# Attention and token mixing on one core: q/k transposes moved to VectorE, 32-row scores, fixed order, resident loads

## The chip, the cores and the metric

The kernel runs on one core of a Trainium2 chip. The metric is the device time of one execution in microseconds (us). A run is called fast when it lies within 1.5% of the fastest run of the same kernel, else slow. This kernel's runs scatter by some per cent (the kernel before: 195.8 to 204.7 us in the rounds of the experiments, at mean granted TensorE clocks of 0.88 to 0.96), so I compare fast runs with fast runs where there are enough of them, and say so where a median includes slow ones.

Engine names as in the profile: PE is TensorE's matmuls, PEld its weight loads, DVE is VectorE, ACT is ScalarE, POOL is GpSimd (which issues the loads), SP is SyncE (which issues the stores of the new kernel; in the kernel before ScalarE does). L12 is line 12 of the kernel in question. The line numbers of the two kernels differ.

## The reference

```python
# q, k, v: (8 batches, 8 heads, 576 rows, 64), float32; attention within chunks of 64 rows
scores = matmul(q_c, k_c.T) / sqrt(64)            # per batch, head, chunk: 64 x 64
x = softmax(scores) @ v_c                         # -> (8, 576, 512), heads side by side
wq, wk = x @ w_q, x @ w_k                         # (8, 576, 64)
mixed = (wq @ wk.T / sqrt(64)) @ x                # (8, 576, 512)
out = relu(mixed) @ w_out                         # float32
```

Both kernels compute `mixed` as `wq @ (wk.T @ x)`; I call `wk.T @ x` "g" (64 x 512). The inputs are random, with a standard deviation of 0.1 for q and k, so scores are small and the softmax is nearly flat. Therefore the comparison with the reference hardly notices wrong scores (experiment 6 shows it).

## The kernel before

Per batch, per pair of heads: load rows as they lie, transpose q and k on PE, scores, exp, attention times v, scaling. The token mixing of the batch before is cut into pieces and put between the head pairs; a scheduler then orders each engine's instructions. All of the token mixing shares two PSUM banks, the pool with tag "m".

```python
    st_psum = ... bufs=2      # scores            (8 PSUM banks used in all)
    x_psum  = ... bufs=2      # attention times v
    t_psum  = ... bufs=2      # q/k transposes
    m_psum  = ... bufs=2      # all of the token mixing, tag "m"
    ...
    # load: q/k rows of 64 elements (256 bytes in DRAM), one DMA per 128 positions
    nc.gpsimd.dma_start(res[ti][0:rows, j], src[b][:, ds(j * P, rows), :].rearrange("h p d -> p h d"))
    ...
            for ti in range(2):                       # q, then k
                tp = t_psum.tile([P, NJ, P], F16, name=f"tp{ti}", tag="tp")
                for j in range(NJ):
                    nc.tensor.transpose(tp[:, j, 0:rows], qn[ti][0:rows, j, 2 * hp : 2 * hp + 2, :], ident[0:rows, 0:rows])
                sb = qkt_pool.tile(...)
                nc.vector.tensor_copy(sb[:], tp...)
            ...
                        nc.tensor.matmul(stp[r0 : r0 + CH, ci, :], lhsT=kt[r0 : r0 + CH, cs], rhs=qt[r0 : r0 + CH, cs])  # 64 rows
    ...
        def p_mixed():
            for i in range(NDC):                      # four pieces
                ma = m_psum.tile([P, 512], F32, name="ma", tag="m")
                mb = m_psum.tile([P, CH], F32, name="mb", tag="m")
                ...                                   # two matmuls, two relus on ScalarE
        def p_out():                                  # five a batch, the last of 64 rows
                op = m_psum.tile([P, DM], F32, name="op", tag="m")
                ...                                   # four matmuls, copy, store
```

The softmax here doesn't subtract the row's maximum and nothing guards it: scores larger than these inputs give would overflow.

## Time and profile before

Median 197.88 us of 4 runs (197.22 to 201.69). From the page of the profiled execution, which spans 195.1 us: the share of each engine, and, in 40 slices, PE's busy tenths and the granted clock.

```profile
span 195.1 us, 4950 instructions
...
PE 165.3 (85%) x2064; PEld 91.6 (47%) x2064; DVE 80.7 (41%) x272; ACT 77.9 (40%) x193; POOL 117.1 (60%) x153
...
PE   0249987999889989988989999999999998975691
...
PEclk9999998557999699999999999999987999998559
...
PE 70%; DMA 10%; ACT 9%; POOL 4%; DVE 4%; issue 2%; POOLq 0%; ACTq 0%; DVEq 0%
```

The last line is the chain that ended last, by engine. The windows of the middle (columns: the stretch, its length, then busy us of PE, PEld, DVE, ACT, POOL, then clock, DMA share and GB/s):

```profile
100.00:120.00 20.00, 19.45 (x275) 11.30 (x275) 10.49 (x38) 9.97 (x25) 17.52 (x23) 1.00 1.89 170
120.00:140.00 20.00, 19.77 (x287) 11.60 (x286) 10.93 (x38) 9.62 (x26) 7.14 (x10) 1.00 1.08 119
```

A matmul counts as busy for its whole duration, about 0.19 us for one of 64 columns although the next may start some 20 ns later (the scores matmuls between 75 and 150 us). So a wait shorter than that leaves no idle time.

Two groups of the page (columns: line, engine, operation, shapes, count; busy us and mean ns; idle time before, and its releaser):

```profile
L188 PE MATMUL op<-wout_133,rmx 128*128 128x512 f16 (+1 forms) x160 | 46.6, 432 | 1.0 <-ACT rmx L174 1.0
...
L174 ACT ACTIVATE rmx<-ma 128x512 f16<-128x512 f32 x32 | 19.2, 600 | 12.2 <-PE mb L173 11.1
```

And PE's wait for the relu of the mixed pieces, from the list of waits (who waited for whom: us in total, times, longest):

```profile
PE ma L172 <- ACT rmx L174: 3.7, 8, 0.7
```

### The profile page before, as it was taken

How to read it: one execution, taken by the hardware profiler on the slowest of the kernel's cores; microseconds unless marked ns; L12 is line 12 of the kernel's file. 1: busy time of each engine (PE TensorE's matmuls, PEld its weight loads, DVE VectorE, ACT ScalarE, POOL GpSimd, SP SyncE). 2: the span in 40 equal slices, each digit the busy share in tenths (PEclk: the TensorE clock that was granted, in tenths of full speed). 3: DMA queues.
4: the chain of work that ended last, by engine and by line, in shares of the span. 5: the costliest groups of instructions: out<-in, count | busy, mean ns of one | idle time of the engine just before them, and what ended most of it. 6: DMA issues, size and time to landing. Idle time of an engine off the chain costs nothing.

```text
span 195.1 us, 4950 instructions
## 1 busy us (share of the span) xinstructions
PE 165.3 (85%) x2064; PEld 91.6 (47%) x2064; DVE 80.7 (41%) x272; ACT 77.9 (40%) x193; POOL 117.1 (60%) x153
## 2 busy tenths in 40 slices
PE   0249987999889989988989999999999998975691
PEld 0127742445545446544655475556554654442230
DVE  0025840453745337433846275618640764160000
ACT  2002213433326533563338543661464326623432
POOL 8999996999999997799799499703000000000000
PEclk9999998557999699999999999999987999998559
DMA  5999999999999999999999999975002300240015
GB/s 36 133 134 95 152 155 125 100 145 207 216 171 141 108 205 223 138 119 212 229 144 147 226 162 151 133 230 61 5 0 110 127 12 0 90 155 0 0 64 178
DMA packets 119749, 24.56 MB, mean 126 GB/s; under 512 B 114608, under 2 KB 115120, under 8 KB 119728
## 3 DMA queue, kind: packets, MB, share of 16 engines
q0 software_dynamic: 114480, 14.82, 117.6%
q10 hardware_dynamic: 5248, 9.44, 13.7%
q8 instruction: 16, 0.26, 0.6%
q14 instruction: 5, 0.04, 0.1%
HBM read 29.62 MB, written 9.44 MB: 200 GB/s over the span
## 4 chain that ended last, share of the span: by engine, by line
PE 70%; DMA 10%; ACT 9%; POOL 4%; DVE 4%; issue 2%; POOLq 0%; ACTq 0%; DVEq 0%
PE op L188 17%; DMA out_dram<-osb 8%; PE ma L172 7%; PE tx L109 6%; PE gp L154 6%; PE wpa L120 4%; ACT rmx L174 3%; DMA qn_102<-in_q_dram 2%; POOL qn_102 L72 2%; ACT osb L196 2%; ACT wqkT L135 2%; POOL qn_103 L72 2%; PE wknp L145 2%; DVE x_nat L281 1%; PE wpb L127 1%
## 5 line engine op out<-in xcount | busy, mean ns | idle before, releaser
L83 POOL DMA_DIRECT2D vt<-in_v_dram x64 | 47.7, 807 | 15.7 <-PE stp_2655 L245 7.7
L188 PE MATMUL op<-wout_133,rmx 128*128 128x512 f16 (+1 forms) x160 | 46.6, 432 | 1.0 <-ACT rmx L174 1.0
L196 ACT COPY osb<-op 128x512 f32<-128x512 f32 (+1 forms) x40 | 23.3, 583 | 33.1 <-PE op L188 25.8
L188 PEld LDWEIGHTS <-rmx 128*128 128x128 f16 (+1 forms) x160 | 16.0, 110 | 19.8 <-issue 9.6
L174 ACT ACTIVATE rmx<-ma 128x512 f16<-128x512 f32 x32 | 19.2, 600 | 12.2 <-PE mb L173 11.1
L270 PEld LDWEIGHTS <-est 64*64 64x64 f16 x640 | 15.8, 115 | 11.2 <-issue 4.7
L109 PE MATMUL tx<-ident,x_nat 128*128 128x128 f16 x160 | 14.9, 231 | 4.7 <-ACT osb L196 1.8
L109 PEld LDWEIGHTS <-x_nat 128*128 128x128 f16 x160 | 10.2, 101 | 7.2 <-issue 4.4
L135 ACT CAST wqkT<-wpa 128x512 f16<-128x512 f32 x8 | 4.7, 585 | 19.5 <-PE wpb L127 19.5
L154 PE MATMUL gp<-x_nat,wkn 128*64 128x512 f16 (+1 forms) x40 | 11.4, 389 | 1.2 <-DVE wkn L149 1.2
L223 PE MATMUL tp_192<-ident,qn_102 128*128 128x128 f16 (+1 forms) x5 | 1.4, 277 | 6.9 <-DMA qn_102<-in_q_dram 6.8
L177 ACT ACTIVATE rmx<-mb 128x64 f16<-128x64 f32 x32 | 7.2, 224 | 0.0
L154 PEld LDWEIGHTS <-wkn 128*64 128x64 f16 (+1 forms) x40 | 3.5, 107 | 6.5 <-DVE wkn L149 1.6
L223 PEld LDWEIGHTS <-qn_102 128*128 128x128 f16 (+1 forms) x20 | 1.9, 115 | 8.9 <-DMA qn_102<-in_q_dram 7.6
L252 ACT ACTIVATE est<-stp_209 128x320 f16<-128x320 f32 x1 | 0.4, 437 | 13.0 <-PE stp_209 L245 13.0
L72 POOL DMA_DIRECT2D qn_136<-in_k_dram x5 | 5.4, 1085 | 0.0
L72 POOL DMA_DIRECT2D qn_135<-in_q_dram x5 | 5.4, 1081 | 0.0
L229 DVE COPY qkt_198<-tp_192 128x576 f16<-128x576 f16 x1 | 0.5, 458 | 11.9 <-PE tp_192 L223 11.9
L145 PE MATMUL wknp<-ident,wqkT 64*128 64x64 f16 (+1 forms) x40 | 3.4, 196 | 2.0 <-ACT wqkT L135 1.8
L72 POOL DMA_DIRECT2D qn_1309<-in_k_dram x5 | 4.4, 873 | 1.2 <-DMA vt<-in_v_dram 1.2
L149 DVE COPY wkn<-wknp 128x256 f16<-128x256 f16 x8 | 2.3, 288 | 6.5 <-PE wknp L145 6.4
L72 POOL DMA_DIRECT2D qn_102<-in_q_dram x5 | 4.5, 904 | 0.3 <-issue 0.3
(656 smaller groups left out, 384.0 us busy)
## 6 DMA issues: line engine op xcount, KB each, us to landing
out_dram<-osb ACTq DMA_DIRECT2D x32, 256.0 KB, 4.0
vt<-in_v_dram POOLq DMA_DIRECT2D x64, 72.0 KB, 4.5
out_dram<-osb ACTq DMA_DIRECT2D x8, 128.0 KB, 3.7
qn_102<-in_q_dram POOLq DMA_DIRECT2D x4, 128.0 KB, 4.0
qn_103<-in_k_dram POOLq DMA_DIRECT2D x4, 128.0 KB, 4.2
wout_133<-in_moe_w_out_dram POOLq DMA_DIRECT2D x1, 512.0 KB, 6.3
qn_135<-in_q_dram POOLq DMA_DIRECT2D x4, 128.0 KB, 6.4
qn_136<-in_k_dram POOLq DMA_DIRECT2D x4, 128.0 KB, 6.4
```

Source lines behind the costliest of these rows:

```text
L72: nc.gpsimd.dma_start(res[ti][0:rows, j], src[b][:, ds(j * P, rows), :].rearrange("h p d -> p h d"),)
L83: nc.gpsimd.dma_start(vt[CH * hh : CH * hh + CH, :, 0:CH], v[b, 2 * hp + hh].rearrange("(c kk) d -> kk c d", kk=CH),)
L109: nc.tensor.transpose(tx[:, j, :], x_nat[:, j, ts(i, P)], ident[:])
L120: nc.tensor.matmul(pa[:, :], lhsT=wqk16[:, i, :], rhs=xts[i][:, 0:512], start=(i == 0), stop=(i == NDC - 1),)
L135: nc.scalar.copy(wqkT[:, 0:512], pa[:, :])
L145: nc.tensor.transpose(wknp[0:rows, j, :], wkT[:, ds(j * P, rows)], ident[CH:P, CH:P])
L154: nc.tensor.matmul(gp[:, :], lhsT=wkn[0:kk, j, :], rhs=x_nat[0:kk, j, :], start=(j == 0), stop=(j == NJ - 1),)
L172: nc.tensor.matmul(ma[:, :], lhsT=g16[:, ts(i, P)], rhs=wqT[:, 0:512])
L174: nc.scalar.activation(rmx[:, i, 0:512], ma[:, :], AF.Relu, scale=scale_moe)
L188: nc.tensor.matmul(op[0:m, :], lhsT=rmx[:, i, ds(st * P, m)], rhs=wout16[:, i, :], start=(i == 0), stop=(i == NDC - 1),)
L196: nc.scalar.copy(osb[0:m, :], op[0:m, :])
L270: nc.tensor.matmul(xp[hh][half : half + CH, sl // 2, 0:65], lhsT=est[r0 : r0 + CH, c, :], rhs=vt[r0 : r0 + CH, c, 0:65], start=True, stop= ...
```

## The change

The intent: take the 320 q/k transposes (40 a batch) off PE. Two consecutive rows of q or k are loaded as one 512-byte run, and VectorE's transpose is given pairs of fp16 elements, treated as fp32, in an access pattern laid out for blocks of 32 x 32. The transposed operand then has 32 rows, with even and odd elements interleaved along the columns, so each scores product becomes two accumulated 32-row matmuls, spread over four row tiles. The two PSUM banks of the transposes go to the output projection. All loads are resident (no buffer is reused), the program order of every engine is fixed as written, and output tiles run over pairs of batches (36 full tiles instead of 32 full and 8 half ones). wk is computed directly in the layout that g needs, without transposes. g and mixed are split into two column or row halves. There are six output staging buffers instead of three, and their stores are issued from SP.

The core of the diff (cut):

```diff
+    ctx.enter_context(tc.manual_schedule())               # each engine in written order
+    def load_qk(b, part):                                 # all batches issued at the start
+            nc.gpsimd.dma_start(dst[b][part][:],
+                src[b].rearrange("(t p r) d -> p t (r d)", p=P, r=R)[:, a:e, :])
+    st = ps.tile([P, 2, 512], F32, name="st")             # four tiles of two banks, each single
+    xp = ps.tile([P, 2, 512], F32, name="xp")
+    mp = ps.tile([P, 2, 512], F32, name="mp")
+    op = ps.tile([P, 2, 512], F32, name="op")
+    def tr(b, part):
+            nc.vector.transpose(out=o.rearrange("p (t w r) -> p t r w", r=R, w=32),
+                in_=src[b][part].bitcast(F32).rearrange("p t (r d) -> p t r d", d=32))
-                    nc.tensor.transpose(tp[:, j, 0:rows], qn[ti][...], ident[...])
+            for e in range(2):
+                for i in range(4):
+                    nc.tensor.matmul(st[half : half + CH, i // 2, ...],
+                        lhsT=operand(kT, b, t, i, e), rhs=operand(qT, b, t, i, e),
+                        start=(e == 0), stop=(e == 1))
+    def mix(b, i, half):                                  # 2 banks of mp, one relu over both
+        for h in range(2):
+            nc.tensor.matmul(mp[:, h, 0:HS], lhsT=g16[...], rhs=wqT[...], start=True, stop=True)
+        nc.scalar.activation(rmx[...], mp[:, :, 0:HS], AF.Relu, scale=scale_moe)
+    def o_(cnt=1):                                        # one output tile, banks in turn
+                nc.tensor.matmul(op[:, n % 2, :], lhsT=rmx[...], rhs=wout[:, i, :], ...)
+            nc.scalar.copy(os_[:], op[:, n % 2, :])
+            nc.sync.dma_start(of[n * P : n * P + P, :], os_[:])
+    # loop, p = b - 1: scores(b,0) attend(p,3) xtr(p,2) o_ scores(b,1) attend(b,0) xtr(p,3) o_ wq wk
+    #   scores(b,2) attend(b,1) g o_ scores(b,3) attend(b,2) tr(b+1,0) mix mix o_ mix mix
+    #   xtr(b,0) o_ xtr(b,1) tr(b+1,1)
```

## The prediction

> **What bounds it now.** TensorE. The span is 195.1 us; the page has PE busy 85%, and 70% of the chain that ended last is on PE. The windows from 100 to 140 us have PE busy 19.5 to 19.8 of 20 us at full clock. DVE (41%) and ACT (40%) are not limits. In the timeline, the starts of neighbouring matmuls between 75 and 150 us give a batch's cost by group, 20.8 us in all: output projection 5.2, q/k transposes 5.2 (80 of them, 66 ns apart, 160 ns where the array changes shape), scores 2.4, attention times v 2.2, g 1.1, mixed 1.7, x transposes 1.3, wq/wk 1.25, wk transposes 0.4. Loads lead except at the start: attention reads v at about 17 us. From 176 us PE waits on ACT in turns, at a clock near 0.54.
>
> **What the change does, a batch.**
> - Removes 80 q/k transposes: -5.2 us of PE.
> - Adds four fp32 VectorE transposes of 576 elements. [...]
> - Doubles the scores matmuls to 144, of 32 rows. Two 64-row tiles now start a matmul every 16 to 20 ns. [...]
> - wk made directly (20 matmuls, about 30 ns each) in place of transposes; [...] mixed on two row halves; 36 full output tiles instead of 40: 3.9 us. PE work: about 12.5 us.
> - Fixed order and single PSUM buffers turn saving into waits. Each mixed piece fills both banks of one tile, so the next waits for a relu of 576 columns (512 took 0.60 us): about 1 us a round, four rounds, one covered by an output tile; the last also holds up the x transposes. With waits before wq and scores: 3.5 to 4.5 us a batch.
>
> A steady batch costs 16.5 to 17 us against 20.8. PE issue plus PE-ACT turns set it, no longer PE alone.
>
> **Loads.** A 256-byte source row costs 14 to 16 ns per engine (landings 0.85 to 1.05 us apart per 1024 rows). From the w_out load I estimate 23 ns for 512 bytes. A batch needs 11 us, all are in by 95 us: no limit in the steady state. But v of batch 0, one load, lands near 15 us, and batch 1 waits for loads until about 28 us.
>
> **Sum.** v at 15, batch 0 to 19, batch 1 to 43, six batches of 17 to 146, the last mixing chain to 158, five output tiles and the store to 167 at a low clock: span 167, time 170 us.
>
> Predicted 170 us, 80% range 157 to 184. Faster by over 2%: 0.93; within 2%: 0.04; slower: 0.03.
>
> **What would show it.** No PE transposes of q and k; [...] PE busy share 65 to 75%, with mixed waiting for relu the largest PE wait; first attention near 15 us.
>
> **What would make it wrong.** [...] a clock that falls because PE rests more; smaller waits than I count (-8 us).

The sum came to about 12.5 us of PE work and 16.5 to 17 us in all for a batch, a span of 167 us and a time of 170 us. Of the terms, two are counts times spacings of the trace before: 4.5 output tiles a batch of four starts, 216 ns each, are 3.9 us, and the starts of 64-column matmuls over 128 rows, with which I priced wk, lie 29 to 39 ns apart there. The 23 ns for a 512-byte run was an estimate from the w_out load; in the first 51 us of the trace after, each load of 1152 such runs of k lands 1.44 to 1.71 us after that of q, which on 16 DMA engines is 20 to 24 ns a run.

## The result, and the profile after

Median 178.87 us of 4 runs (177.65 to 179.53), all fast. The ratio to the kernel before is 0.909, 95% interval 0.900 to 0.919. Ratios and intervals are from fast runs alone, so not quite the ratio of the medians that I quote (0.904 here). The prediction was 170 us with 157 to 184: inside the range, with the gain a third smaller than forecast (19.0 us instead of 28).

The page after, same lines as before:

```profile
span 177.6 us, 5290 instructions
...
PE 117.6 (66%) x2400; PEld 71.8 (40%) x2400; DVE 74.3 (42%) x149; ACT 70.0 (39%) x117; POOL 49.5 (28%) x49
...
PE   0024350693998499759964988589578957955861
...
PEclk9999999996599569987998899789969996996555
...
PE 44%; DVE 17%; ACT 17%; DMA 14%; issue 4%; POOL 2%; ACTq 0%; POOLq 0%
```

PE fell from 85% to 66% busy, and the chain no longer lies mostly on it. The same two windows, where the clock was 1.00 and now is 0.91:

```profile
100.00:120.00 20.00, 15.98 (x381) 9.96 (x378) 11.83 (x24) 10.53 (x18) 0.00 (x0) 0.91 0.25 85
120.00:140.00 20.00, 16.07 (x367) 10.46 (x369) 10.46 (x21) 9.49 (x16) 0.00 (x0) 0.91 0.21 79
```

The groups that answer to those of before, with the new scores and transposes:

```profile
L254 PE MATMUL op<-wout,rmx 128*128 128x512 f16 x144 | 47.5, 462 | 3.1 <-ACT osb L262 3.1
...
L236 ACT ACTIVATE rmx<-mp 128x576 f16<-128x576 f32 x32 | 20.9, 653 | 10.0 <-PE mp L228 9.9
...
L134 PE MATMUL st<-qT,kT 32*64 32x64 f16 x1152 | 17.9, 209 | 9.5 <-DVE kT L118 8.6
...
L118 DVE STREAM_TRANSPOSE qT<-qn 128x576 f32<-128x576 f32 x16 | 12.4, 772 | 9.3 <-DMA qn<-in_q_dram 9.3
```

And PE's waits for the relu, from the list of waits (the second is that of the x transposes, which come next in the same banks):

```profile
PE mp L228 <- ACT rmx L236: 17.2, 21, 1.0
...
PE mp L181 <- ACT rmx L236: 5.2, 7, 0.7
```

One transpose of q takes 0.77 us on average. Waiting of mixed pieces for the relu is the largest wait of PE, 17.2 us in 21 waits, as forecast; before it was 3.7.

**Where the time came from.** A milestone that both kernels have is the end of the multiply that completes a batch's attention (the last write of `x_nat`, `xn`, read from the timeline):

| | batch 1 complete | batch 7 complete | end of the span | per batch between |
|---|---|---|---|---|
| before | 53.8 us | 172.0 us | 195.1 us | 19.7 us |
| after | 49.8 us | 151.9 us | 177.6 us | 17.0 us |
| difference | -4.0 | -16.1 more | +2.6 given back | -2.7 |

So, in these two traces, the whole gain is in the start and the steady batches; the tail is longer. Next, the pieces of my own sum:

| step of the forecast | forecast | measured in the profile after |
|---|---|---|
| first attention (v of batch 0 there) | 15 us | 15.4 us |
| passes 0 and 1 of the loop end (the next scores start) | 19 and 43 us | 24.6 and 46.9 us |
| six more passes of 17 us | to 146 us | 17.2 us each, to 150.3 us |
| last mixing chain | to 158 us (12) | to 161.6 us (11.3) |
| last five output tiles and store | to 167 us (9) | to 177.6 us (16.0) |

The steady pass was right. The start was 3.9 us too short and the tail 7 us too short; both can be read.

**The tail.** The chain of waits, in order of time, for two of the last five output tiles (start, us, what):

```profile
164.21 1.88 PE op L254 x4
166.09 0.03 ACTq L262
166.12 0.04 issue
166.16 0.59 ACT osb L262
166.75 0.04 issue
166.79 1.88 PE op L254 x4
```

Each tile starts 2.58 us after the one before: matmuls, then the copy of *that* tile, then the next matmuls, although the next tile writes the other bank. And the four matmuls take 1.88 us because the clock is at half for the last 17 us (within a tile they start 378 to 427 ns apart there, and 216 ns at full clock). My sum assumed two banks used in turn.

**The steady pass.** One mixing stage on PE (start, us, engine, line, operation, tiles, shapes, count, idle before):

```profile
108.99 0.30 PE L228 MATMUL mp<-wqT,g 64*128 64x288 f16 x2
110.12 0.30 PE L228 MATMUL mp<-wqT,g 64*128 64x288 f16 x2 [0.83 <-ACT rmx L236]
110.35 1.04 PE L254 MATMUL op<-wout,rmx 128*128 128x512 f16 x4
111.32 0.30 PE L228 MATMUL mp<-wqT,g 64*128 64x288 f16 x2
112.66 0.30 PE L228 MATMUL mp<-wqT,g 64*128 64x288 f16 x2 [1.04 <-ACT rmx L236]
113.70 0.69 PE L181 MATMUL mp<-ident,xn 128*128 128x128 f16 x5 [0.74 <-ACT rmx L236]
114.19 1.91 PE L254 MATMUL op<-wout,rmx 128*128 128x512 f16 x4
```

Three waits, 2.6 us, as the single buffer implies. Then the next output tile takes 1.91 us instead of 1.04: the clock has fallen from 1.00 to 0.50. The windows, cut at the change of the clock, show the stretch of waits and the slow stretch next to each other:

```profile
106.30:109.70 3.40, 2.99 (x108) 1.77 (x96) 1.95 (x5) 2.33 (x5) 0.00 (x0) 1.00 0.02 6
109.70:113.10 3.40, 1.80 (x10) 0.70 (x10) 1.83 (x3) 2.26 (x5) 0.00 (x0) 1.00 0.25 98
113.10:116.50 3.40, 2.80 (x14) 1.54 (x13) 0.49 (x1) 0.87 (x2) 0.00 (x0) 0.50 0.15 56
```

After a stretch with PE busy 1.80 of 3.40 us, the next 3.4 us run at half clock. This recurs once a pass, at 79.0, 96.0, 113.1, 130.2 and 147.2 us (and for 6.8 us at 41.4 and 58.5); PE was busy for 0.9 to 1.8 us of the 3.4 before each of the five. It is not peculiar to this kernel. In all fourteen traces the clock's record changes on a grid of 3.41 us. I cut them along it, from the first entry of each record on: of the 48 stretches at full clock with PE busy for less than 1.8 us, 44 were followed by half clock; of the 276 with more than 2.6 us, 8 were. Between the two it went either way. In the trace after, all six with at most 1.8 us were followed by half clock, and none of the 17 with more than 2.6. (The first entry there is at 38.0 us. Before it the page prints full clock, but groups of scores matmuls start 13.0 to 13.2 ns apart, as they do at half clock at 46.9 us, against 8.2 at full clock. So I read no clock there.) In this stage, then, the relu waits come with a second cost: 2.6 us of waits, and behind them an output tile slower by 0.87 us.

### The profile page after: what moved, and what is told of

It reads as the page before. It is cut to its first block, busy times and chain, and to the rows that moved or that the text cites. A ratio compares the mean times of both kernels' runs of the same rounds, so it can differ in the third digit from the quotient of the medians.

```text
span 177.6 us, 5290 instructions
## 1 busy us (share of the span) xinstructions
PE 117.6 (66%) x2400; PEld 71.8 (40%) x2400; DVE 74.3 (42%) x149; ACT 70.0 (39%) x117; POOL 49.5 (28%) x49
## 4 chain that ended last, share of the span: by engine, by line
PE 44%; DVE 17%; ACT 17%; DMA 14%; issue 4%; POOL 2%; ACTq 0%; POOLq 0%
PE op L254 19%; ACT rmx L236 10%; DMA kn<-in_k_dram 8%; DVE xn L169 7%; DMA vt<-in_v_dram 6%; PE mp L189 6%; PE mp L181 5%; ACT osb L262 5%; PE mp L228 4%; DVE xt L184 4%; PE xp L159 3%; PE mp L217 3%; PE op L203 3%; DVE kT L118 3%; DVE qT L118 2%
## 5 line engine op out<-in xcount | busy, mean ns | idle before, releaser
L254 PE MATMUL op<-wout,rmx 128*128 128x512 f16 x144 | 47.5, 462 | 3.1 <-ACT osb L262 3.1
L262 ACT COPY osb<-op 128x512 f32<-128x512 f32 x36 | 21.1, 586 | 48.1 <-PE op L254 42.5
L142 ACT ACTIVATE est<-st 128x640 f16<-128x640 f32 (+1 forms) x32 | 20.9, 652 | 29.1 <-PE st L134 28.9
L184 DVE COPY xt<-mp 128x640 f16<-128x640 f16 x32 | 15.5, 485 | 34.6 <-PE mp L181 34.6
L169 DVE TENSOR_TENSOR xn<-xp,rec 128x640 f16<-128x640 f32 x32 | 26.4, 824 | 1.1
L181 PE MATMUL mp<-ident,xn 128*128 128x128 f16 x160 | 19.1, 268 | 9.8 <-ACT rmx L236 5.2
L236 ACT ACTIVATE rmx<-mp 128x576 f16<-128x576 f32 x32 | 20.9, 653 | 10.0 <-PE mp L228 9.9
L134 PE MATMUL st<-qT,kT 32*64 32x64 f16 x1152 | 17.9, 209 | 9.5 <-DVE kT L118 8.6
L228 PE MATMUL mp<-wqT,g 64*128 64x288 f16 x64 | 10.4, 307 | 18.1 <-ACT rmx L236 17.2
L67 POOL DMA_DIRECT2D qn<-in_q_dram x16 | 16.1, 1005 | 18.8 <-DMA vt<-in_v_dram 16.7
L181 PEld LDWEIGHTS <-xn 128*128 128x128 f16 x160 | 14.4, 120 | 16.0 <-issue 14.2
L67 POOL DMA_DIRECT2D kn<-in_k_dram x16 | 16.0, 1001 | 8.8 <-DMA qn<-in_q_dram 4.5
L73 POOL DMA_DIRECT2D vt<-in_v_dram x8 | 14.7, 1834 | 4.3 <-DMA kn<-in_k_dram 4.0
L159 PEld LDWEIGHTS <-est 64*64 64x64 f16 x576 | 10.0, 119 | 14.0 <-issue 12.2
(22 smaller groups left out, 46.9 us busy)
```

The lines of the kernel that those rows point to most:

```text
L67: nc.gpsimd.dma_start(dst[b][part][:], src[b].rearrange("(t p r) d -> p t (r d)", p=P, r=R)[:, a:e, :],)
L134: nc.tensor.matmul(st[half : half + CH, i // 2, (t - a) * CH : (t - a) * CH + CH], lhsT=operand(kT, b, t, i, e), rhs=operand(qT, b, t, i, ...
L142: nc.scalar.activation(est[b % 2][s].rearrange("p i t c -> p i (t c)")[:, :, 0:n], st[:, :, 0:n], AF.Exp, scale=scale_attn,)
L159: nc.tensor.matmul(xp[CH * (c % 2) : CH * (c % 2) + CH, hh, jj * 66 : jj * 66 + 65], lhsT=est[b % 2][s][half : half + CH, i // 2, t - SETS ...
L169: nc.vector.tensor_tensor(out=xn[b % 2][:, :, 2 * kk * D : 2 * kk * D + 2 * D].rearrange("p j (i d) -> p i j d", i=2), in0=xpv[:, :, :, 0: ...
L181: nc.tensor.transpose(tx[:, j * P : j * P + P], xn[b % 2][:, j, i * P : i * P + P], ident[:])
```

## The experiments

Twelve kernels ran. The kernel before in the same rounds took 196.7 to 203.6, 195.8 to 204.7 and 199.0 to 202.5 us on the three chips. Its medians there, 199.6 to 200.5 us, are about 1% above the 197.88 of the first round, so a difference of 2 us or less against another round says nothing. Unless I say otherwise, differences are against the new kernel's 178.87. Every run passed the comparison with the reference.

### 1. The two banks of the output projection as two tiles

```diff
-    op = ps.tile([P, 2, 512], F32, name="op")
+    op = [ps.tile([P, 512], F32, name=f"op{i}") for i in range(2)]
```
(and `op[:, n % 2, :]` becomes `op[n % 2][:]`)

> The two PSUM banks of the output projection become two tiles; nothing else. Theory A: in the new kernel each of the last five output tiles waits for the copy of the tile just before it (starts 2.58 us apart: 1.86 us of matmuls at half clock, then 0.59 us of copy), although that copy reads the other bank, because the waits are kept for the whole two-bank tile. Then the starts of the last tiles come 1.9 us apart or less, the time falls by 3 to 6 us against the new kernel's 178.9 (to 173 to 176). Rival B: the tail is set by the clock alone and the banks are already used in turn: starts stay 2.5 us apart, time within 1 us of 178.9.

Measured: median 172.27 us of 4 runs; the one fast run 168.28, the other three 171.75 to 173.93, all below the new kernel's lowest. The profiled run is one of the slow ones (172.79), so I read only its tail. From its timeline, the matmuls and the copies (other engines left out):

```profile
160.66 6.19 PE L254 MATMUL op<-wout,rmx 128*128 128x512 f16 x20
...
161.98 0.59 ACT L262 COPY osb<-op 128x512 f32<-128x512 f32 x1 [0.57 <-PE op L254]
...
163.69 0.59 ACT L262 COPY osb<-op 128x512 f32<-128x512 f32 x1 [1.12 <-PE op L254]
165.19 0.59 ACT L262 COPY osb<-op 128x512 f32<-128x512 f32 x1 [0.91 <-PE op L254]
166.05 0.59 ACT L262 COPY osb<-op 128x512 f32<-128x512 f32 x1 [0.28 <-PE op L254]
```

The twenty matmuls now run without a wait, 6.2 us instead of 12.2. The half clock, which in the new kernel lasts to the end, lasts 3.4 us here: the copies start 1.7, 1.5 and then 0.9 us apart. By the milestone the tail is 19.2 us instead of 25.7, and what comes before it is within 0.5 us of the new kernel. Theory A holds: the waits had been kept for the whole two-bank tile, and this alone was worth 6.6 us by medians (slow runs included; the one fast run is 9.4 us below the new kernel's lowest), with the clock's return in it.

### 2. Mixed pieces over two pairs of banks, relu shared by ScalarE and VectorE

```diff
+        bk = mp if i == 0 else op                 # both split into one-bank tiles, as in 1
-        nc.scalar.activation(rmx[...][:, i, :, o : o + HS], mp[:, :, 0:HS], AF.Relu, scale=scale_moe)
+        nc.scalar.activation(rmx[...][:, i, o : o + HS], bk[0][:, 0:HS], AF.Relu, scale=scale_moe)
+        nc.vector.tensor_scalar(out=rmx[...][:, 2 + i, o : o + HS], in0=bk[1][:, 0:HS],
+            scalar1=scale_moe, scalar2=0.0, op0=ALU.mult, op1=ALU.max)
```
(the output tile between the pieces and `tr(b+1,0)` move behind them)

> As e1, and the other two-bank tile is split too; the four mixed pieces of a batch alternate between two pairs of banks, and each piece's relu is shared: one bank by ScalarE, one by VectorE; the next batch's first transposes and the output tile that stood between the pieces move behind them. Theory A: the steady batch of 17.1 us holds about 3 us of PE waiting for relu, so a batch falls to 14 to 15.5 us and the time by 12 to 20 us against 178.9, with PE waiting for relu under 5 us in all (17.2 now), and fewer half-clock windows. Rival B: PE work alone sets the batch, or VectorE becomes the limit: batch stays above 16.3 us, and time falls only by what e1 gives.

Measured: 154.48 us, ratio to before 0.778 (0.761 to 0.795). By the milestone, a batch takes 14.8 us instead of 17.0. The waits of mixed pieces for a relu, of either engine, fall from 17.2 to 6.1 us (I expected under 5). In the steady part, half-clock stretches are left at 85.5 and 102.6 us. The four pieces of one mixing stage now start within 1.6 us, as against 3.7 with an output tile among them; PE in the timeline:

```profile
100.58 0.30 PE L228 MATMUL mp<-wqT,g 64*128 64x288 f16 x2
100.71 0.29 PE L228 MATMUL op<-wqT,g 64*128 64x288 f16 x2
101.37 0.28 PE L228 MATMUL mp<-wqT,g 64*128 64x288 f16 x1 [0.37 <-ACT rmx L236]
102.18 0.28 PE L228 MATMUL mp<-wqT,g 64*128 64x288 f16 x1 [0.54 <-DVE rmx L239]
102.19 0.74 PE L228 MATMUL op<-wqT,g 64*128 64x288 f16 x2
```

The gain is 24 us, more than I expected, and theory A holds with its size too small: I had not counted that the clock and the tail recover as well (experiment 1, about 6.6 us, is contained in it). The second pair of banks, the shared relu and the moved instructions came together; no run separates them.

### 3. Scores without the round over four row tiles

```diff
-            for e in range(2):
-                for i in range(4):
+            for i in range(4):
+                for e in range(2):
```

> Order of the scores matmuls only: both halves of one 32-row tile one after the other, instead of going round the four row tiles. Theory A: the round-robin order lets four row tiles run together (starts 9 to 11 ns apart now); with pairs on one row tile fewer overlap, starts go to 15 to 25 ns apart, 1 to 2 us a batch, time up by 5 to 14 us. Rival B: the queue of the engine overlaps them anyway or instruction issue sets the pace: starts stay near 10 ns and the time within 2 us.

Measured: 178.52 us: no change. Starts of scores matmuls in a group at full clock are 8.5 to 9.4 ns apart on average, 8.2 in the new kernel. Theory A fails: the order of the row tiles does not matter. Whether tiles run together is not shown by this pair, since neighbours still lie on different tiles half of the time; the order as such buys nothing. The 64-row products of before started 16.3 to 16.4 ns apart in unbroken groups at full clock (20 ns on average between 75 and 150 us), so two 32-row ones in 16.4 ns cost no more than one did.

### 4. Every VectorE transpose done twice

```diff
-        for src, dst in ((qn, qT), (kn, kT)):
+        for src, dst in ((qn, qT), (kn, kT), (qn, qT), (kn, kT)):
```

> Each VectorE transpose is done twice, with the same result. Adds 3.0 us of VectorE work a batch (four more of 0.76 us), 24 us in all. Theory A: in the steady batch VectorE is 9 to 10 of 17 us busy and the transposes are off the critical path, so most of it hides: time up by 2 to 8 us (some of it at the start, where VectorE's order puts them before work that PE waits for). Rival B: VectorE's fixed order puts the transposes on the path: time up by 18 to 26 us.

Measured: 184.5 us, 5.6 us more, for 24 us of added VectorE work:

```profile
L118 DVE STREAM_TRANSPOSE qT<-qn 128x576 f32<-128x576 f32 x32 | 24.1, 753 | 6.7 <-DMA qn<-in_q_dram 6.7
```

(The line is that of q, half of which is added; that of k has 23.8 us, so 24 us are added in all.) Theory A holds: three quarters of it hides. The transposes are mostly off the critical path.

### 5. The new kernel without the fixed order

```diff
-    ctx.enter_context(tc.manual_schedule())
```

> The new kernel without the fixed order: one line taken out, so the compiler's scheduler may reorder each engine's instructions. Theory A: the written order is what hides the single buffers; a free order brings no gain: time within 3% of 178.9, or slower. Rival B: the fixed order is what causes the PE waits (mixed on relu, attention behind transposes that wait for loads); a free order recovers 5 us or more.

Measured: 165.09 us, 13.8 us faster. Rival B: with these single buffers the written order loses against the scheduler's. Waits of mixed pieces for their relu, to compare with 17.2 us in the new kernel, and of output tiles, which are still there because the tiles are still whole:

```profile
PE op L253 <- ACT osb L261: 3.7, 8, 0.7
...
PE mp L227 <- ACT rmx L235: 2.6, 5, 1.0
```

The scheduler puts other work of PE between the pieces, and the mean clock is 0.93 instead of 0.87. But this is only part of the gain: by the milestone, 5.5 us of it come before batch 1 is complete (44.3 us instead of 49.8), 7.1 us in the next six batches (15.8 us each instead of 17.0) and 2.1 us in the tail.

### 6. The kernel before without its transposes on PE

The q/k rows are copied instead of transposed; the result is wrong.

```diff
-                    nc.tensor.transpose(tp[:, j, 0:rows], qn[ti][...], ident[...])
-                nc.vector.tensor_copy(sb[:], tp.rearrange("p a c -> p (a c)")[:, 0:S])
+                nc.vector.tensor_copy(sb[:], qn[ti].rearrange("p a h d -> p (a h d)")[:, 0:S])
```

> The kernel before with the q/k transposes of TensorE left out and the loaded rows copied instead (wrong result on purpose; loads, copies, matmuls else unchanged). Theory A: PE issue sets the kernel before, so 5.2 us a batch, 35 to 42 us in all, goes: about 158 to 165 us, below the new kernel's 178.9, which would show that the rewrite lost a good part of that gain to waits. Rival B: the waits between engines come up as PE's work goes, or the loads become the limit (11.7 to 14 us a batch): under 25 us goes, 173 us or more.

(The 11.7 to 14 us of loads are an estimate from the landings of the trace before: a batch is 13.5 times 1024 rows, at the 0.85 to 1.05 us of the prediction, which gives about 11.5 to 14.2.)

Measured: 193.27 us, ratio to before 0.970 (0.955 to 0.984). Of the 42 us that I had put down to the transposes (5.2 us a batch), 6 show. Rival B, far beyond its bound. The same two windows:

```profile
100.00:120.00 20.00, 17.13 (x226) 9.67 (x225) 10.46 (x36) 8.50 (x21) 18.45 (x24) 0.83 2.00 176
120.00:140.00 20.00, 17.67 (x236) 9.31 (x237) 10.52 (x36) 9.81 (x25) 7.98 (x11) 0.83 1.14 122
```

PE has 18% fewer matmuls in these windows and is still 86 to 88% busy, at a clock of 0.83 where it had 1.00. Between 75 and 150 us, 30 of 70 starts of neighbouring matmuls of the output projection are 425 to 428 ns apart, the spacing at half clock, where before it was 6 of 61, the others mostly 215 to 216. So part of the work removed came back as slower matmuls, and the rest, which I have not itemised, as waits, of which some may hide inside matmul durations (about 0.19 us each). PE's own work, taken alone, did not set the kernel before.

### 7. Loads and transposes of the start in another order

```diff
     for b in range(1, B):
         load_qk(b, 0)
+        if b == 1: (load w_q, w_k here, no longer before batch 1)
         load_v(b)
         load_qk(b, 1)
+        if b == 1: (load w_out here)
...
-        if b + 1 < B:
+        if 0 < b and b + 1 < B:
             tr(b + 1, 1)
+        if b == 1: tr(1, 1)                        # just before scores(1, 2)
```

> The new kernel with the weights loaded after the first half of q/k of batch 1 (w_out after the second), and the second pair of transposes of batch 1 done later in VectorE's order, just before the scores that need them. Theory A: PE waits at the start because the loads of weights (3.2 us) stand before q/k of batch 1, and because a transpose that waits for its load stands before the scaling that attention waits for (PE idle 26.9 to 31.7 us): batch 2 starts at about 41 to 44 us instead of 46.9, time falls by 3 to 6 us. Rival B: the loads' total bytes set the start whatever their order: under 1.5 us.

Measured: 173.43 us, 5.4 us faster; batch 2's scores start at 41.4 us instead of 46.9. Theory A holds, at the upper end. The start held two misplaced things, moved here together, so that their shares stay open: weights in front of batch 1's q/k, and, in VectorE's fixed order, a transpose that waits for its load in front of the scaling that attention waits for.

### 8. Output tiles per batch instead of per pair

```diff
-            pr, tl = n // NCH, n % NCH
+            bb, tl = n // NJ, n % NJ
+            m = P if tl < NJ - 1 else CH
```

> The new kernel with output tiles per batch (four of 128 rows and one of 64), 40 instead of 36. Theory A: each extra tile costs its four matmuls and a shape change, 0.95 us, in the steady batch: half a tile more a batch, time up by 2 to 5 us, and no more than that. Rival B: the output tiles fill time in which PE waits anyway: within 1 us.

(The 0.95 us are an estimate from the trace before: four starts of 216 ns, and about 0.09 us for the shape, since from a 128-row transpose to a 64-row one it was 152 ns from start to start where equal ones had 55 to 67.)

Measured: 179.83 us (fast runs 177.88 and 178.41). Rival B: forty tiles cost no more than thirty-six. That the output tiles stood where PE would have waited is the likely reason, not a shown one: the waits of mixed pieces for the relu fall only from 17.2 to 15.1 us, and the clock of the profiled run is 0.90 instead of 0.87, which can hide a small cost.

### 9. Experiment 6, with the freed banks for the output projection

```diff
-    t_psum = ctx.enter_context(tc.tile_pool(name="tps", bufs=2, ...
+    o_psum = ctx.enter_context(tc.tile_pool(name="ops", bufs=2, ...
-                op = m_psum.tile([P, DM], F32, name="op", tag="m")
+                op = o_psum.tile([P, DM], F32, name="op", tag="o")
```

> e6 (the kernel before without its q/k transposes on TensorE, wrong on purpose) kept its 20 us a batch. Here the two PSUM banks that the transposes no longer use hold the output projection, which so far shares two banks with everything else of the token mixing. Theory A: the kernel before is held by the chain of x transposes, wq/wk, g, mixed and output tiles through those two banks, each of which waits for a copy; with banks of its own for the output projection a batch falls to 15 to 18 us and the time to 160 to 180 us. Then what the rewrite gained came from the banks that it freed more than from PE time. Rival B: the loads or the order hold e6: within 4 us of e6's 193.

Measured: 182.7 us; the one fast run 178.87, the others 182.4 to 183.8. Against the fast runs of experiment 6 (190.9 to 193.6, on another chip) that is 12 to 15 us less: the same PE work, with two more PSUM banks for the token mixing, gains twice what removing the transposes alone did. The median is just outside theory A's range and the fast run inside. By the milestone of the profiled run, one of the slow ones, a batch takes 18.9 us on average over the six, and 15.5 to 18.4 only in the last three. So theory A is supported in its direction, not as the whole cause.

### 10. The kernel before with three banks for the token mixing, one for the transposes

```diff
-    t_psum = ... bufs=2        m_psum = ... bufs=2
+    t_psum = ... bufs=1        m_psum = ... bufs=3
```

> The kernel before, complete and correct, with one of the two banks of the q/k transposes given to the shared pool of the token mixing (three there, one here). Theory A (the shared pool holds it): faster by 2 to 6%, 188 to 195 us. Rival B: no change or slower, since the transposes now wait for their copies and PE's work is the same: 197 us or more.

Measured: 205.74 us (one fast run 198.23, three slow ones 204.3 to 208.2; before 199.0 to 202.5). Rival B: the fast run is within 1 us of the lowest of the kernel before, so nothing was gained. A third bank taken from the transposes does not pay while they stay on PE. The trace is of a slow run (208.23; a batch takes 21.6 us in it) and I read no more from it.

### 11. Everything together

Experiments 1, 2 and 7, and from batch 2 on:

```diff
             scores(b, 2)
             attend(b, 1)
+        if 2 <= b and b + 1 < B:
+            tr(b + 1, 0)
```

> The new kernel with e1, e2 and e7 together, and from batch 2 on the first transposes of the next batch placed just after the second attention group, where VectorE has time. If the tail, the relu waits and the start are separate losses, e7's 5.4 us comes off e2's 154.5, and the 1 us a batch that e2's scores wait for these transposes comes off too: 143 to 150 us. If the start of e2 is hidden by something else: 152 us or more.

Measured: 148.62 us, ratio to before 0.741 (0.734 to 0.749), fast runs 147.04 to 149.19, mean clock 0.94 to 0.98. Within the range that I gave. It is 5.9 us below experiment 2 by medians. Between the two profiled runs (8.1 us apart in span), 3.4 us lie in the start, 3.3 in the next six batches (14.3 us each instead of 14.8) and 1.4 in the tail. So the three losses add up in the main, but both the start (5.4 expected) and the moved transposes (1 us a batch expected) gave less than they should have. This version beats both kernels. Its page, with the clock full nearly throughout:

```profile
span 144.9 us, 5349 instructions
...
PE 107.6 (74%) x2400; PEld 66.8 (46%) x2400; DVE 86.2 (59%) x181; ACT 62.0 (43%) x125; POOL 49.5 (34%) x49
...
PEclk9999999999999986999999969999999999999999
```

### 12. Experiment 11 without the fixed order

```diff
-    ctx.enter_context(tc.manual_schedule())
```

> e11 without the fixed order. e5 showed that the free order beats the written one by 14 us when the buffers are single. Theory A: it did so by filling the waits for relu and for copies; with those gone it has nothing left to fill: within 4% of e11, either way. Rival B: the free order is better in general: 5% or more below e11.

Measured: 155.78 us, ratio to before 0.775, so 4.6% above experiment 11's 0.741. Slightly outside what theory A allows, and the opposite of rival B. The two traces show where the 7.3 us between their spans lie: in one batch. Batch 2 takes 23.1 us from milestone to milestone instead of 15.2; batches 3 to 7 take 69.6 us together instead of 70.6, and both tails are 16.2 us. In that batch the scheduler had put a transpose, which waits for its load, in front of the copy of wk, whose matmuls had ended at 46.6 us:

```profile
50.13 0.78 DVE L119 STREAM_TRANSPOSE qT<-qn 128x576 f32<-128x576 f32 x1 [4.19 <-DMA qn<-in_q_dram]
50.83 0.45 DVE L210 CAST wkn<-op 128x320 f16<-128x320 f32 x1
```

PE waited 4.0 us for that copy, and the clock was at half from 50.3 to 64.0 us. It is the kind of fault that experiment 7 mended in the written order. So the two orders are alike in the later batches, and this pair does not show that a written order is better as such. Nor do experiments 5 and 12 together show that single buffers were what spoiled it: between them the written order was mended too (experiment 7, the moved transposes).

## Why the prediction was right, and where not

The time lay in the range, for reasons that hold in part.

- **"PE issue plus PE-ACT turns set it", 16.5 to 17 us a batch.** Right: 17.0 us by the milestone, with the relu of the mixed pieces as PE's largest wait (17.2 us). Experiment 2 took most of those waits away, and a batch fell to 14.8 us.
- **Transposes on VectorE.** Measured: 0.74 to 0.78 us each, mostly off the path, since doubling them cost 5.6 of 24 us.
- **Scores starts.** Measured: 8.2 ns apart at full clock. The round over four row tiles is not what does it: without it they were 8.5 to 9.4 ns apart, and the time was the same (experiment 3).
- **"36 full output tiles instead of 40: 3.9 us".** Forty cost no more time (experiment 8).
- **"What bounds it now. TensorE."** This step failed. I read 85% busy and 19.8 of 20 us as PE being the limit, and took 5.2 us a batch as the value of removing the transposes. Experiment 6 removed them and 6 of 42 us showed. (The count of 80 is wrong as well: there are 40 a batch, 117 ns from one start to the next one on PE between the milestones of batches 2 and 6, so 4.7 us. The conclusion is the same.) The sum for the new kernel did not use that difference, as it was made from the new order's own waits, so the total survived a wrong reading of the old kernel. The prediction's 20.8 us a batch was a sum of start-to-start times over a cut window; the milestone gives 19.7, so the steady saving is 2.7 us a batch and not 4.
- **"Five output tiles and the store to 167 at a low clock".** The mis-sized term, 16.0 us measured for 9. I took the two banks as two buffers; the waits treated them as one. Experiment 1 took 6.6 us of it back.
- **"Batch 1 waits for loads until about 28 us ... batch 1 to 43".** 3.9 us too short: v of batch 1 landed at 26.6 us, but the second part of its k only at 29.9, and the scaling waited behind that transpose until 30.6. Experiment 7 recovered 5.4 us there.
- **A clock that falls because PE rests more** I had named as a risk; it is in the trace once a pass, half clock for 3.4 us after a stretch with PE busy for 0.9 to 1.8 us of 3.4.

What stays open: what holds experiment 6 at 193 us. The clock (0.83 for 1.00 in the middle) and the shared PSUM banks (experiment 9) each account for a part; I have no run that separates the rest, which may be the scheduler's order. A further candidate stands in its trace, untested: the three output staging buffers. Its ScalarE copies wait 9.3 us in seven waits for a store to free one (6.4 us in four in the kernel before, none in the new kernel, which has six), and 18.3 us of the chain that ended last are such stores in the middle of the run, pieces of 3.4 to 5.3 us. The two-row loads were not tried alone. How the gain of 19 us of the whole rewrite divides among freed banks, transposes and order is not settled either; experiment 5 says that the fixed order, as written, took away 14, about 5.5 of it at the start.

## What to carry to other kernels

A busy PE is not a PE that sets the time (97 to 99% busy in the middle of the kernel before, and 6 of 42 us showed): before crediting a change with the PE work that it removes, take that work away alone and see what the clock and the waits give back. Count buffers as the waits see them, by tile and not by bank (2.58 us from one of the last tiles to the next with one tile of two banks, 0.9 to 1.7 with two tiles, in experiment 1), and look for the place where one relu or copy stands between two matmuls of the same tile; in experiment 2 filling such gaps took PE's waits of mixed pieces for a relu from 17.2 to 6.1 us, and the mean clock of the profiled run rose from 0.87 to 0.95. Where an order is fixed, by hand or by a scheduler, look for an instruction that waits for a load and stands in front of work that others wait for: it cost 5 us at the start of the new kernel, together with the weights, and it opens the one batch in which experiment 12 lost its 7 us.
